# Small softmax sums for every pair of heads, and a last batch whose keys and gates stay in SBUF

## The chip, the cores and the metric

The kernel runs on one core of a Trainium2 chip. TensorE (PE in the profile) multiplies matrices into PSUM, VectorE (DVE), ScalarE (ACT) and GpSimd (POOL) do the elementwise work, and SyncE (SP) issues the transfers. The metric is the device time of one execution in microseconds; lower is better.

## The reference

Three layers follow each other on 4 batches, 12 heads, 448 tokens and 64 channels a head (768 in all).

```python
# 1. attention, for each batch and head
scores = cap * tanh(q @ k.T / 8 / cap)
attn = exp(scores - max) / (sum + 1e-9)
x = attn @ v                                  # heads side by side: [4, 448, 768]
# 2. token shift and a gated product
xk = mu_k * x + (1 - mu_k) * x_prev
xr = mu_r * x + (1 - mu_r) * x_prev
k = max(xk @ w_k, 0)                          # [4, 448, 1024], the "keys"
v = (k * k) @ w_v
x = v * sigmoid(xr @ w_r)                     # xr @ w_r are the "gates"
# 3. rotation, mixing of tokens, mixing of channels
theta = x @ w_theta
y = w_tok_r @ (x * cos(theta)) + w_tok_i @ (x * sin(theta))
u = x + y
out = u + max(u @ w_ch, 0)
```

## The kernel before

All data stand with channels on the partitions and the 448 tokens along the free axis. The products of the second and third layer are made from fp16 halves: each fp32 operand is split into a high and a low half, and three fp16 matmuls of 448 columns (high by high, high by low, low by high) stand for one product. In each batch the keys (`kmm`, 8 output tiles) and the gates (`rmm`, 6) take 6 blocks of channels each, the products with w_v (`vmm`, 6 tiles) take 8, `thm` (w_theta, 6 tiles) 6, `tmm` (tokens, 6 tiles) 7, `cmm` (w_ch, 6 tiles) 6.

Attention runs over 24 pairs of heads, pair g in batch g // 6. `scores` makes the scores, `tanh` and `exp`; `attend` adds up the four blocks of keys, divides, and splits the result into the halves that `kmm` and `rmm` read. There are two ways to divide, switched by `WIDE = 12`:

- `narrow`, pairs 0 to 11: 16 small matmuls of 112 columns sum the weights of one head and one quarter of the tokens each, so that one tile of 112 columns holds all sums (8 groups of 16 rows). VectorE takes the reciprocal of 112 columns, and 4 matmuls of 112 columns (`spread`) hand each quarter back to all channels. The output of `av` is copied to SBUF (`avo`) and multiplied there.
- `wide`, pairs 12 to 23: two additions on half the partitions each (`fold`) bring in the last block of keys, two matmuls of 448 columns give each channel its sum, VectorE takes the reciprocal of 448 columns, and one instruction multiplies the output of `av` by it straight from PSUM.

A weight matrix comes in as float64 words and goes through `group` (or `tokens` for the two token matrices): a load into one of the two buffers `w_s`; `rebase` and three bit operations that make an fp32 tile `f` (`f_s` has 3 such tiles; `tokens` uses 7 of the 9 tiles `xf_s`); `squares`, an ACT instruction that sums the squares for the scale and writes its unused output into the load buffer `w`; a small matmul, three tiny operations; and the two halves (`whi`, `wlo`).

The keys and gates of every batch are stored to DRAM (`kd`, `zd`). `values(b)` later loads the keys back through the four tiles `ka_s`, splits them into `k2_s` (8 tiles), multiplies them by w_v, loads the gates through the five tiles `z_s`, applies the sigmoid, multiplies, and stores the result to DRAM (`xd`). The products with w_v are taken in the order of the batches 0, 1, 2, 3.

`Plan` orders all this before anything runs: each operation has a rank, one or more engines with a planned duration, and the buffers it reads and writes; `order` simulates the engines, always takes the ready operation of least rank, and writes out one fixed order of instructions for each engine. A pool made with `fifo` hands out its buffers in the order in which the program names them. `o_r2`, `o_l2` mark the points where the memory of attention, and later of the first products, is given to new tiles: `o_r2` waits for the last multiplication of attention, `o_l2` for the last key and gate product.

Of the kernel before, what the change touches and what calls it, by code (L numbers as in the profile page):

```python
# [7 lines left out]
F32 = mybir.dt.float32  # L8
# [16 lines left out]
SH = S // 2  # L25
SQ = S // 4
# [4 lines left out]
KT = 7  # L31
# [217 lines left out]
def v1(n):  # L249
    return 0.17 + n / 940.0  # L250
# [6 lines left out]
def act(n):  # L257
    return 0.17 + n / 1150.0
# [19 lines left out]
def body(nc, tc, exact, qk, v, cap, mu_k, mu_r, w_k, w_v, w_r, w_th, w_tr, w_ti, w_ch, out):  # L278
# [4 lines left out]
    WIDE = 12  # L283
# [80 lines left out]
    wk, wr, wv, wt, wc = ([Buf() for _ in range(n)] for n in (1, 1, 2, 1, 1))  # L364
    wo = [Buf() for _ in range(KT)]
# [149 lines left out]
    def group(rank, src, dst, m, inv, nb, after=(), early=False):  # L515
# [44 lines left out]
    for b in range(B):  # L560
        R = (2 * NP * b - 7.1) * SLOT if b else 3
        vb = v[NP * b:NP * b + NP].rearrange("g p n -> (g p n)").rearrange("(p n) -> p n", p=128)
        parts = []
        n = 2 * DM
        for c in range(2):
            t = Buf(w_s)
            op("DMA", 0.03 + n / 700, R - 10, lambda t=t, c=c, vb=vb: nc.sync.dma_start(out=t.t, in_=vb[:, c * n:(c + 1) * n]), w=[t], after=[o_open1], name="ldm")
            parts.append([(t, lambda t=t: t.t, n, 128)] if b == 0 else (t, lambda t=t: t.t, n, t))
# [100 lines left out]
    def narrow(A, x, sxb, th, vn, z, sp, rs, ps):  # L669
# [11 lines left out]
        op("PE", 0.74, A, sums, r=[z, th[3]], w=[sp], name="sums")  # L681
# [11 lines left out]
        op("PE", 0.8, A + 2, spread, r=[rs], w=[sp], name="spread")  # L693
# [12 lines left out]
    def wide(A, x, sxb, th, vn, z, sp, ps):  # L706

        rs = lambda: x.t[:, 1:S + 1]

        def sums():  # L710
            for h in range(2):
                nc.tensor.matmul(sp.t[64 * h:64 * h + 64, 0:S], unit.to_broadcast([128, D]), z.t[:, h], start=True, stop=True, skip_group_check=True)  # L712
        op("PE", 0.74, A, sums, r=[z], w=[sp], name="sums")

        def den():
            if exact:
                nc.vector.tensor_scalar(out=rs(), in0=sp.t[:, 0:S], scalar1=1e-9, scalar2=None, op0=ALU.add)
            nc.vector.reciprocal(out=rs(), in_=rs() if exact else sp.t[:, 0:S])  # L718
        op("DVE", 2.95, A + 1, den, r=[sp], w=[x], name="den")

        def av():
            for c in range(3):
                for h in range(2):
                    nc.tensor.matmul(ps.t[64 * h:64 * h + 64, 0:S], vn.t[0][:, h, c], th[c].t[:, h], start=(c == 0), stop=False, skip_group_check=True)  # L724
            for i in range(2):
                for h in range(2):
                    nc.tensor.matmul(ps.t[64 * h:64 * h + 64, SH * i:SH * i + SH], vn.t[1][:, i, h], th[3].t[:, h], start=False, stop=True, skip_group_check=True)
        op("PE", 3.02, A + 0.5, av, r=[vn, *th], w=[ps], name="av")
        last1.append(op("DVE", v1(S) + 0.06, A + 4, lambda: nc.vector.scalar_tensor_tensor(
            out=x.t[:, 1:S + 1], in0=ps.t[:, 0:S], scalar=sxb.t, in1=rs(), op0=ALU.mult, op1=ALU.mult), r=[ps, sxb], w=[x], name="norm"))  # L730

    def attend(g):
# [8 lines left out]

        if g >= WIDE:
            for i in range(2):
                p, q = slice(64 * i, 64 * i + 64), slice(SH * i, SH * i + SH)
                op(tt(S), 0, A - 1 + 0.5 * i, lambda e, p=p, q=q: e.tensor_tensor(out=z.t[p, :, q], in0=z.t[p, :, q], in1=th[3].t[p], op=ALU.add), r=[th[3]], w=[(z, i)], name="fold")
            wide(A, x, sx[b], th, vn, z, sp, ps)
        else:
            narrow(A, x, sx[b], th, vn, z, sp, rs, ps)
# [25 lines left out]
    gone, gone_v, kend = [], [], []  # L774
# [14 lines left out]
    for b in range(B):  # L789
        def taps(i):  # L790
            return [((hi, lo), lambda hi=hi: hi.t, lambda lo=lo: lo.t) for hi, lo in (mixed[i, b, j] for j in range(KD))]
        for m, ps in units("kmm", b, wk, KF, taps(0), PAIR * NP * (b + 1), gone, PAIR * NP / 14):
            a = Buf(g_s)
            op("ACT", act(S) + 0.05, 0.0, lambda ps=ps, a=a, b=b, m=m: nc.scalar.activation(out=a.t, in_=ps.t[:, 0:S], func=AF.Relu, scale=kap[b].t[:, m:m + 1]),  # L794
               r=[ps, (kap[b], m)], w=[a], name="kev")
# [8 lines left out]
            kend.append(op("DMA", 0.65, 0.0, lambda a=a, t=kd[b][m]: nc.sync.dma_start(out=t.t, in_=a.t), r=[a], w=[kd[b][m]], name="dst"))  # L804
        for m, ps in units("rmm", b, wr, KD, taps(1), PAIR * NP * (b + 1 + KF / 14), gone, PAIR * NP / 14):
            o_ = Buf(tmp_s)
            op({"ACT": act(S), "DVE": 0.62}, 0, 0.0, lambda e, ps=ps, o_=o_: copy(e, o_.t, ps.t[:, 0:S]), r=[ps], w=[o_], name="zev")
            op("DMA", 0.65, 0.0, lambda o_=o_, t=zd[b][m]: nc.sync.dma_start(out=t.t, in_=o_.t), r=[o_], w=[zd[b][m]], name="dst")
# [7 lines left out]
    z_s, k2_s, xs_s, xg_s, xf_s, uh_s = Slots(5, True), Slots(8, True), Slots(12, True), Slots(2, True), Slots(9, True), Slots(9, True)  # L816
    CSN, ZBN, ZTN = 3, 2, 3
    cs_s, zb_s, zt_s = Slots(CSN, True), Slots(ZBN, True), Slots(ZTN, True)
    ka_s = Slots(4, True)
    q_ps, e_ps = Slots(3, True), Slots(2, True)  # L820

    def open_r2():
        live["r"].release()
        live["p"].release()
        p2 = live["p"] = tc.alloc_tile_pool(name="psum3", bufs=1, space=PSUM)
        q = tiles(p2, 4, [128, 512], F32, "q")
        q_ps.tiles, e_ps.tiles = [q[0], q[1], one[0]], q[2:]
        r2 = live["r"] = tc.alloc_tile_pool(name="r2", bufs=1, side="right")
        wt[0].tile = r2.tile([128, KD, 2, DM], F16, name="wt")
        for i, bf in enumerate(wo):  # L830
            bf.tile = r2.tile([128, 2, S], F16, name=f"wo{i}")
        ka_s.tiles = tmp2 + tiles(r2, 2, [128, S], F32, "ka")
        k2_s.tiles = tiles(r2, k2_s.n, [128, 2, S], F16, "k2")
        xf_s.tiles = tiles(r2, xf_s.n, [128, S], F32, "xf")
        xg_s.tiles = tiles(r2, xg_s.n, [128, S], F32, "xg")
# [16 lines left out]
    o_r2 = op("SYS", 0.0, 0, open_r2, after=last1)  # L852
# [10 lines left out]
    def tokens(rank):  # L863
        fo = []
        for i in range(KT):
# [12 lines left out]
            fo.append((f, fv, S, raw))  # L878
        size(rank, squares(rank, fo, small(KT)), io, 0, so)
# [52 lines left out]
    for b in range(B):  # L932
        values(b)
# [159 lines left out]
```

## Time and profile before

| | us |
|---|---|
| median of 3 runs | 805.9 (805.28 to 806.34) |
| profiled execution, its own time | 805.84 |
| its span, first to last instruction | 804.0 |
| TensorE busy | 770.6 (96% of the span) |
| VectorE busy | 563.6 (70%) |
| ScalarE busy | 440.8 (55%) |
| GpSimd busy | 92.6 (12%) |
| bytes moved by DMA | 114.76 MB, 143 GB/s on average |

The busy time of TensorE counts the full latency of each matmul, and those of neighbours overlap, so the distance between the starts of two instructions says more than the length of one. An idle time in square brackets behind an instruction names what ended it.

### The profile page before, as it was taken

What the parts mean: (1) busy time and instruction counts of PE and PEld (TensorE: products, weight loads), DVE (VectorE), ACT (ScalarE), POOL (GpSimd) and SP (SyncE); (2) the same over time, 40 slices, a digit from 0 to 9 for tenths busy, and PEclk for the clock granted to TensorE, in tenths of its full rate; (3) what the DMA queues carried; (4) which work ended last, traced back from release to release, by engine and by line L of the source; (5) the groups of instructions that cost most, each with busy time, mean ns of one, the idle gap of its engine ahead of it and who ended that gap; (6) DMA issues with size and microseconds to landing.
All of it is one profiled execution on the core that took longest, in us unless ns stands there. A gap on an engine that the chain in (4) does not pass through costs nothing.

```text
span 804.0 us, 12769 instructions
## 1 busy us (share of the span) xinstructions
PE 770.6 (96%) x4924; PEld 386.0 (48%) x4924; DVE 563.6 (70%) x1014; ACT 440.8 (55%) x677; POOL 92.6 (12%) x99
## 2 busy tenths in 40 slices
PE   5989999999999999998999889999999999999996
PEld 2445455454444444443555445555555555555553
DVE  2888897967778899879657768966856544645531
ACT  4889877878775875755526434355635333222201
POOL 1214403201130120101001000101201000000000
PEclk9999999999999999999999999999999999999999
DMA  8855455455343434225556866553535333324402
GB/s 258 257 173 181 158 180 191 138 171 184 113 136 99 139 92 157 97 75 172 176 191 221 296 193 203 185 152 84 123 60 136 82 92 92 90 65 98 99 28 73
DMA packets 116829, 114.76 MB, mean 143 GB/s; under 512 B 55820, under 2 KB 108824, under 8 KB 116760
## 3 DMA queue, kind: packets, MB, share of 16 engines
q1 hardware_dynamic: 116592, 113.86, 46.8%
q8 instruction: 40, 0.66, 0.3%
q14 instruction: 29, 0.24, 0.1%
q10 hardware_dynamic: 168, 0.01, 0.0%
HBM read 78.98 MB, written 23.86 MB: 128 GB/s over the span
## 4 chain that ended last, share of the span: by engine, by line
PE 87%; DMA 5%; DVE 4%; ACT 2%; issue 1%; SPq 1%; ACTq 0%; DVEq 0%
PE one L783 12%; PE one L784 11%; PE one L785 11%; PE big L653 7%; PE q L989 4%; PE q L987 4%; PE q L988 4%; PE one L724 4%; PE one L1010 3%; PE one L1009 3%; PE one L1011 3%; PE one L698 3%; PE q L957 2%; PE q L959 2%; PE q L958 2%; DMA w<-in_v 2%
## 5 line engine op out<-in xcount | busy, mean ns | idle before, releaser
L662 ACT ACTIVATE th<-big,tsc 128x896 f32<-128x896 f32 x72 | 70.1, 1002 | 22.6 <-PE big L653 22.4
L653 PE MATMUL big<-qk 64*64 64x448 f32 x576 | 67.8, 571 | 8.2 <-DMA qk<-in_qk 7.7
L783 PE MATMUL one<-k,wv 128*128 128x448 f16 x192 | 68.3, 356 | 6.2 <-DVE z L909 6.2
L666 ACT ACTIVATE th<-th,cap_t 128x896 f32<-128x896 f32 x72 | 73.0, 1039 | 0.0
L783 PE MATMUL one<-sl,wk 128*128 128x448 f16 x192 | 68.5, 357 | 2.4 <-ACT g L794 1.9
L784 PE MATMUL one<-sl,wk 128*128 128x448 f16 x192 | 68.2, 355 | 0.9 <-POOL sl L758 0.9
L784 PE MATMUL one<-k,wv 128*128 128x448 f16 x192 | 68.2, 355 | 0.0
L785 PE MATMUL one<-k,wv 128*128 128x448 f16 x192 | 68.1, 355 | 0.0
L785 PE MATMUL one<-sl,wk 128*128 128x448 f16 x192 | 68.1, 355 | 0.0
L989 PE MATMUL q<-wo,zt 128*128 128x448 f16 x168 | 59.2, 352 | 0.0
L987 PE MATMUL q<-wo,zt 128*128 128x448 f16 x168 | 59.2, 352 | 0.0
L988 PE MATMUL q<-wo,zt 128*128 128x448 f16 x168 | 59.2, 352 | 0.0
L1013 ACT ACTIVATE z<-one,scal 128x448 f32<-128x448 f32 x24 | 15.1, 627 | 71.9 <-PE one L1011 71.9
L783 PE MATMUL one<-sl,wr 128*128 128x448 f16 x144 | 50.9, 354 | 0.0
L785 PE MATMUL one<-sl,wr 128*128 128x448 f16 x144 | 50.7, 352 | 0.0
L784 PE MATMUL one<-sl,wr 128*128 128x448 f16 x144 | 50.7, 352 | 0.0
L973 DVE SCALAR_TENSOR_TENSOR cs<-xf,scal,cs 128x896 f32<-128x896 f32 x24 | 27.6, 1150 | 31.6 <-DMA xf<-xd 24.2
L718 DVE RECIPROCAL xt<-one 128x448 f32<-128x448 f32 x12 | 35.5, 2956 | 14.0 <-PE one L712 14.0
L758 POOL TENSOR_TENSOR sl<-mx,sl 128x448 f16<-128x448 f32 x24 | 29.5, 1230 | 119.2 <-ACT sl L294 100.6
L454 ACT ACTIVATE w<-w 128x768 f32<-128x768 f32 (+2 forms) x26 | 21.4, 823 | 35.0 <-DMA w<-in_w_ch 17.4
L1014 DVE TENSOR_TENSOR xf<-z,xf 128x448 f32<-128x448 f32 x24 | 15.0, 624 | 34.4 <-ACT z L1013 34.2
L991 DVE SCALAR_TENSOR_TENSOR xf<-q,scal,xf 128x448 f32<-128x448 f32 x24 | 16.4, 683 | 31.8 <-PE q L989 31.6
(191 smaller groups left out, 1739.5 us busy)
## 6 DMA issues: line engine op xcount, KB each, us to landing
qk<-in_qk SPq DMA_DIRECT2D x23, 448.0 KB, 3.8
kd<-g SPq DMA_DIRECT2D x32, 224.0 KB, 2.0
vn<-in_v SPq DMA_DIRECT2D x24, 256.0 KB, 2.7
w<-in_v SPq DMA_DIRECT2D x8, 768.0 KB, 6.2
w<-in_w_k SPq DMA_DIRECT2D x8, 768.0 KB, 5.1
w<-in_w_v SPq DMA_DIRECT2D x12, 512.0 KB, 4.4
zd<-tmp SPq DMA_DIRECT2D x24, 224.0 KB, 2.6
z<-zd SPq DMA_DIRECT2D x24, 224.0 KB, 2.9
```

Source lines behind the costliest of these rows:

```text
L653: nc.tensor.matmul(ps.t[o, h, 0:S], t.t[p, 1, 128 * c + 64 * i:128 * c + 64 * i + 64], t.t[p, 0], start=True, stop=True)
L662: op("ACT", act(n * S) + 0.08, A + 1 + 1.8 * c, lambda src=src, th=th: nc.scalar.activation(out=th.t, in_=src(), func=AF.Tanh, scale=tsc), ...
L666: op("ACT", act(n * S) + 0.08, A + 3 + 1.8 * c, lambda th=th: nc.scalar.activation(out=th.t, in_=th.t, func=AF.Exp, scale=cap_t), w=[th], ...
L718: nc.vector.reciprocal(out=rs(), in_=rs() if exact else sp.t[:, 0:S])
L724: nc.tensor.matmul(ps.t[64 * h:64 * h + 64, 0:S], vn.t[0][:, h, c], th[c].t[:, h], start=(c == 0), stop=False, skip_group_check=True)
L758: op(tt(S, True), 0, R + i, lambda e, t=t, hi=hi, lo=lo: e.tensor_tensor(out=lo.t, in0=t.t, in1=hi.t, op=ALU.subtract), r=[t, hi], w=[lo], ...
L783: nc.tensor.matmul(ps.t[:, 0:S], wh, xh(), start=(kk == 0), stop=False)
L784: nc.tensor.matmul(ps.t[:, 0:S], wh, xl(), start=False, stop=False)
L785: nc.tensor.matmul(ps.t[:, 0:S], wl, xh(), start=False, stop=(kk == len(xs) - 1))
L987: nc.tensor.matmul(o, z.t[:, 0, i], wo[i].t[:, 0], start=(i == 0), stop=False)
L988: nc.tensor.matmul(o, z.t[:, 1, i], wo[i].t[:, 0], start=False, stop=False)
L989: nc.tensor.matmul(o, z.t[:, 0, i], wo[i].t[:, 1], start=False, stop=(i == KT - 1))
```

## The change

- `wide` and `WIDE` go. `narrow` is renamed `normal` and serves all 24 pairs. Its planned durations are 0.36 us for the sums and 0.47 us for `spread`, where both were larger.
- The keys of batch 3 stay in SBUF: tiles 0 to 3 in `g_s`, tiles 4 to 7 in `ka_s`. Its gates stay in `xf_s`. Their stores to and loads from DRAM go. To have these tiles, `open_r2` and its mark `o_r2` move up in the program, and the key and gate evacuations of batch 3 wait for `o_r2`.
- The products with w_v are taken in the order 3, 0, 1, 2.
- `squares` writes its unused output into the two halves of the weight tile that are filled afterwards, and no longer into the load buffer, so `w` is free after the third bit operation. For w_theta and the token matrices it now waits for `o_r2`, for w_ch for `o_l2`.

```diff
+K2N = 8
...
-    WIDE = 12
...
-    def squares(rank, parts, d):
+    def squares(rank, parts, d, after=()):
         ps = Buf(c_ps)
-        for a, (f, val, n, dead) in enumerate(parts):
-            op("ACT", act(n) + 0.19, rank, lambda a=a, val=val, n=n, dead=dead: nc.scalar.activation(out=dead.t[:, 0:n], in_=val(), func=AF.Square, accum_out=d.t[:, a:a + 1]),
-               r=[f] if f is not dead else [], w=[dead, (d, a)], name="norm")
+        for a, (f, val, n, dead, place) in enumerate(parts):
+            op("ACT", act(n) + 0.19, rank, lambda a=a, val=val, place=place: nc.scalar.activation(out=place(), in_=val(), func=AF.Square, accum_out=d.t[:, a:a + 1]),
+               r=[f] if f not in dead else [], w=[*dead, (d, a)], after=after, name="norm")
...
-            parts.append((f, val, n, 128 if early else w))
-        size(rank, grams(rank, [parts], small()) if early else squares(rank, parts, small(len(parts))), inv, m, sw)
+            parts.append((f, val, n, 128) if early else (f, lambda val=val: val().rearrange("p (i t n) -> p i t n", i=nb, t=2), n, [(dst[a], (m, 0)), (dst[a], (m, 1))],
+                                                                     lambda a=a: dst[a].t[:, :, :, 128 * m:128 * m + 128].bitcast(F32)))
+        size(rank, grams(rank, [parts], small()) if early else squares(rank, parts, small(len(parts)), after), inv, m, sw)
...
-    def narrow(A, x, sxb, th, vn, z, sp, rs, ps):
+    def normal(A, x, sxb, th, vn, z, sp, rs, ps):
-        op("PE", 0.74, A, sums, r=[z, th[3]], w=[sp], name="sums")
+        op("PE", 0.36, A, sums, r=[z, th[3]], w=[sp], name="sums")
-        op("PE", 0.8, A + 2, spread, r=[rs], w=[sp], name="spread")
+        op("PE", 0.47, A + 2, spread, r=[rs], w=[sp], name="spread")
...
-    def wide(A, x, sxb, th, vn, z, sp, ps):
...
-        if g >= WIDE:
...
-            wide(A, x, sx[b], th, vn, z, sp, ps)
-        else:
-            narrow(A, x, sx[b], th, vn, z, sp, rs, ps)
+        normal(A, x, sx[b], th, vn, z, sp, rs, ps)
...
+    k2_s, xf_s, ka_s = Slots(K2N, True), Slots(9, True), Slots(4, True)
+    kept, gate = [], []
...
+    o_r2 = op("SYS", 0.0, 0, open_r2, after=last1)
...
-            a = Buf(g_s)
+            last = b == B - 1
+            a = Buf(ka_s if last and m > 3 else g_s)
...
-            kend.append(op("DMA", 0.65, 0.0, lambda a=a, t=kd[b][m]: nc.sync.dma_start(out=t.t, in_=a.t), r=[a], w=[kd[b][m]], name="dst"))
+            if last:
+                kept.append(a)
+            else:
+                op("DMA", 0.65, 0.0, lambda a=a, t=kd[b][m]: nc.sync.dma_start(out=t.t, in_=a.t), r=[a], w=[kd[b][m]], name="dst")
...
-            o_ = Buf(tmp_s)
+            o_ = Buf(xf_s if last else tmp_s)
...
+            if last:
+                gate.append(o_)
...
-            fo.append((f, fv, S, raw))
-        size(rank, squares(rank, fo, small(KT)), io, 0, so)
+            fo.append((f, lambda f=f: f.t.rearrange("p (t n) -> p t n", t=2), S, [(wo[i], 0), (wo[i], 1)], lambda i=i: wo[i].t.bitcast(F32)))
+        size(rank, squares(rank, fo, small(KT), [o_r2]), io, 0, so)
...
-    def values(b):
+    def values(b, n):
...
-            a, k = Buf(ka_s), Buf(k2_s)
+            a, k = Buf(ka_s) if n else kept[m], Buf(k2_s)
...
-            z = Buf(z_s)
+            z = Buf(z_s) if n else gate[m]
...
-    for b in range(B):
-        values(b)
+    for turn, b in enumerate((B - 1, *range(B - 1))):
+        values(b, turn)
```

## Rows read from the trace of the kernel before

**Rows 1.** The page's first part: busy us (share of the span) xinstructions.

```profile
PE 770.6 (96%) x4924; PEld 386.0 (48%) x4924; DVE 563.6 (70%) x1014; ACT 440.8 (55%) x677; POOL 92.6 (12%) x99
```

**Rows 2.** Windows by stage: length, busy PE, PEld, DVE, ACT, POOL, PEclk, DMA share, GB/s.

```profile
189.90:363.40 173.50, 172.58 (x1117) 76.10 (x1117) 143.55 (x214) 119.96 (x187) 24.62 (x21) 1.00 0.37 118
363.40:416.70 53.30, 50.19 (x260) 25.91 (x259) 39.65 (x77) 25.02 (x51) 3.59 (x3) 0.97 0.51 170
416.70:486.60 69.90, 62.31 (x332) 32.85 (x330) 48.76 (x105) 32.35 (x54) 5.92 (x9) 0.98 0.74 249
...
545.00:797.90 252.90, 252.90 (x1339) 130.83 (x1336) 135.65 (x205) 87.44 (x136) 10.20 (x6) 1.00 0.37 87
```

**Rows 3.** Waits of PE: us in total, times, longest.

```profile
PE one L783 <- DVE z L909: 6.2, 3, 2.9
...
PE one L783 <- ACT g L794: 1.9, 3, 1.6
PE one L500 <- ACT w L495: 1.4, 1, 1.4
...
PE one L712 <- DVE xt L718: 0.9, 1, 0.9
PE one L784 <- POOL sl L758: 0.9, 1, 0.9
...
PE one L783 <- ACT sl L294: 0.4, 1, 0.4
```

**Rows 4.** Timeline of PE: narrow sums and spread of one pair, then wide sums.

```profile
114.96 0.59 PE L676 MATMUL one<-pz,ones 128*32 128x112 f32 x16
115.36 0.57 PE L680 MATMUL one<-tl,ones 128*32 128x112 f32 x16
115.86 0.36 PE L783 MATMUL one<-sl,wk 128*128 128x448 f16 x1
...
118.71 1.04 PE L692 MATMUL one<-rs,row 128*128 128x112 f32 x8
119.59 0.35 PE L783 MATMUL one<-sl,wk 128*128 128x448 f16 x1
...
223.50 0.97 PE L712 MATMUL one<-pz,unit 128*64 128x448 f32 x4
224.40 0.36 PE L783 MATMUL one<-sl,wk 128*128 128x448 f16 x1
```

**Rows 5.** Groups of VectorE: the two reciprocals.

```profile
L718 DVE RECIPROCAL xt<-one 128x448 f32<-128x448 f32 x12 | 35.5, 2956 | 14.0 <-PE one L712 14.0
...
L687 DVE RECIPROCAL rs<-one 128x112 f32<-128x112 f32 x12 | 10.2, 852 | 2.9 <-PE one L680 2.7
```

**Rows 6.** Timeline of all engines, 363 to 375: the last pair's division and what follows.

```profile
363.54 2.96 DVE L718 RECIPROCAL xt<-one 128x448 f32<-128x448 f32 x1 [1.44 <-PE one L712]
...
368.33 0.68 DVE L755 SCALAR_TENSOR_TENSOR mx<-mx,mu,xt 128x448 f32<-128x448 f32 x1
...
373.94 0.58 PE L784 MATMUL one<-sl,wk 128*128 128x448 f16 x1
...
374.31 0.58 PE L785 MATMUL one<-sl,wk 128*128 128x448 f16 x1
```

**Rows 7.** Timeline of all engines, 466 to 485: a late load of w_ch.

```profile
468.34 0.38 SPq L530 DMA_DIRECT2D w<-in_w_ch  x1
...
476.00 0.91 ACT L454 ACTIVATE w<-w 128x768 f32<-128x768 f32 x1 [5.74 <-DMA w<-in_w_ch]
...
482.07 0.67 DVE L909 SCALAR_TENSOR_TENSOR z<-one,scal,z 128x448 f32<-128x448 f32 x1
```

**Rows 8.** Waits of ACT: us in total, times, longest.

```profile
ACT z L907 <- DMA z<-zd: 25.6, 13, 4.3
...
ACT w L454 <- DMA w<-in_w_ch: 17.4, 6, 5.7
```

**Rows 9.** Instructions on xf, 380 to 470: ns min/median/max, first and last start.

```profile
L467 DVE SCALAR_TENSOR_TENSOR xf<-w,xf x7: 619/625/630, 394.6 to 422.4; 128x448 uint32<-128x448 uint32 x7
```

More of the change, by code (lines that the diff above doesn't have):

```diff
@@ L362, in body @@
     rs_s = Slots(2, True)
-    wk, wr, wv, wt, wc = ([Buf() for _ in range(n)] for n in (1, 1, 2, 1, 1))
-    wo = [Buf() for _ in range(KT)]
+    wk, wr, wv, wc = ([Buf() for _ in range(n)] for n in (1, 1, 2, 1))
     junk = cpool.tile([128, 128], BF16, name="junk")
@@ L567, in body @@
             op("DMA", 0.03 + n / 700, R - 10, lambda t=t, c=c, vb=vb: nc.sync.dma_start(out=t.t, in_=vb[:, c * n:(c + 1) * n]), w=[t], after=[o_open1], name="ldm")
-            parts.append([(t, lambda t=t: t.t, n, 128)] if b == 0 else (t, lambda t=t: t.t, n, t))
+            parts.append([(t, lambda t=t: t.t, n, 128)] if b == 0 else (t, lambda t=t: t.t, n, [t], lambda t=t: t.t))
         size(R, squares(R, parts, small(2)) if b else grams(R, parts, small()), small(), 0, sv[b])
@@ L704, in narrow @@
         last1.append(op("DVE", v1(S), A + 6, lambda: nc.vector.tensor_tensor(out=x.t[:, 1:S + 1], in0=x.t[:, 1:S + 1], in1=sp.t[:, 0:S], op=ALU.mult), r=[sp], w=[x], name="norm"))
-    def wide(A, x, sxb, th, vn, z, sp, ps):
[L708 to L730, printed above, removed]
     def attend(g):
@@ L772, in body, with open_r2 @@
     attend(NG - 1)
-    gone, gone_v, kend = [], [], []
+    gone = []
+    k2_s, xf_s, ka_s = Slots(K2N, True), Slots(9, True), Slots(4, True)
+    kept, gate = [], []
+    q_ps, e_ps = Slots(3, True), Slots(2, True)
+    wt, wo = [Buf()], [Buf() for _ in range(KT)]
+    def open_r2():
+        live["r"].release()
+        live["p"].release()
+        p2 = live["p"] = tc.alloc_tile_pool(name="psum3", bufs=1, space=PSUM)
+        q = tiles(p2, 4, [128, 512], F32, "q")
+        q_ps.tiles, e_ps.tiles = [q[0], q[1], one[0]], q[2:]
+        r2 = live["r"] = tc.alloc_tile_pool(name="r2", bufs=1, side="right")
+        wt[0].tile = r2.tile([128, KD, 2, DM], F16, name="wt")
+        for i, bf in enumerate(wo):
+            bf.tile = r2.tile([128, 2, S], F16, name=f"wo{i}")
+        ka_s.tiles = tmp2 + tiles(r2, 2, [128, S], F32, "ka")
+        k2_s.tiles = tiles(r2, k2_s.n, [128, 2, S], F16, "k2")
+        xf_s.tiles = tiles(r2, xf_s.n, [128, S], F32, "xf")
+        xg_s.tiles = tiles(r2, xg_s.n, [128, S], F32, "xg")
+    o_r2 = op("SYS", 0.0, 0, open_r2, after=last1)
     def units(name, b, w, n, xs, rank, done, step=1.0):
@@ L792, in body @@
         for m, ps in units("kmm", b, wk, KF, taps(0), PAIR * NP * (b + 1), gone, PAIR * NP / 14):
-            a = Buf(g_s)
+            last = b == B - 1
+            a = Buf(ka_s if last and m > 3 else g_s)
             op("ACT", act(S) + 0.05, 0.0, lambda ps=ps, a=a, b=b, m=m: nc.scalar.activation(out=a.t, in_=ps.t[:, 0:S], func=AF.Relu, scale=kap[b].t[:, m:m + 1]),
-               r=[ps, (kap[b], m)], w=[a], name="kev")
+               r=[ps, (kap[b], m)], w=[a], after=[o_r2] if last else [], name="kev")
             def sq(e, a=a, b=b, m=m):
@@ L815, in body @@
     T2 = 2000.0
-    z_s, k2_s, xs_s, xg_s, xf_s, uh_s = Slots(5, True), Slots(8, True), Slots(12, True), Slots(2, True), Slots(9, True), Slots(9, True)
+    z_s, xs_s, xg_s, uh_s = Slots(5, True), Slots(12, True), Slots(2, True), Slots(9, True)
     CSN, ZBN, ZTN = 3, 2, 3
     cs_s, zb_s, zt_s = Slots(CSN, True), Slots(ZBN, True), Slots(ZTN, True)
[L819 to L835, printed above, removed]
     def open_l2():
@@ L850, in open_u @@
         uh_s.tiles = [w[i // 3][:, i % 3] for i in range(6)] + [la.tile([128, 2, S], F16, name=f"f{i}_u", tag=f"f{i}") for i in range(f_s.n)]
-    o_r2 = op("SYS", 0.0, 0, open_r2, after=last1)
     o_l2 = op("SYS", 0.0, 0, open_l2, after=gone)
@@ L896, in values @@
         for m in range(KF):
-            a, k = Buf(ka_s), Buf(k2_s)
+            a, k = Buf(ka_s) if n else kept[m], Buf(k2_s)
             k2.append(((k,), lambda k=k: k.t[:, 0], lambda k=k: k.t[:, 1]))
-            rk = K20 + 100 * b + m
-            op("DMA", 0.65, rk - 100, lambda a=a, t=kd[b][m]: nc.sync.dma_start(out=a.t, in_=t.t), r=[kd[b][m]], w=[a], after=[o_r2], name="lda")
+            rk = K20 + 100 * n + m
+            if n:
+                op("DMA", 0.65, rk - 100, lambda a=a, t=kd[b][m]: nc.sync.dma_start(out=a.t, in_=t.t), r=[kd[b][m]], w=[a], after=[o_r2], name="lda")
             op(cs(S), 0, rk, lambda e, a=a, k=k, b=b: copy(e, k.t[:, 0], a.t, sa[b].t), r=[a, sa[b]], w=[(k, 0)], after=[o_r2], name="k2h")
@@ L903, in values @@
                 out=k.t[:, 1], in0=a.t, scalar=sa[b].t, in1=k.t[:, 0], op0=ALU.mult, op1=ALU.subtract), r=[a, (k, 0), sa[b]], w=[(k, 1)], name="k2l")
-        for m, ps in units("vmm", b, wv, KD, k2, VM0 + VM1 * b, []):
-            z = Buf(z_s)
-            op("DMA", 0.65, T2 - 110, lambda z=z, t=zd[b][m]: nc.sync.dma_start(out=z.t, in_=t.t), r=[zd[b][m]], w=[z], after=[o_l2], name="ldz")
-            op("ACT", act(S) + 0.1, 1605.2 + 100 * b, lambda z=z, b=b, m=m: nc.scalar.activation(out=z.t, in_=z.t, func=AF.Sigmoid, scale=rho[b].t[:, m:m + 1]),
+        for m, ps in units("vmm", b, wv, KD, k2, VM0 + VM1 * n, []):
+            z = Buf(z_s) if n else gate[m]
+            if n:
+                op("DMA", 0.65, T2 - 110, lambda z=z, t=zd[b][m]: nc.sync.dma_start(out=z.t, in_=t.t), r=[zd[b][m]], w=[z], after=[o_l2], name="ldz")
+            op("ACT", act(S) + 0.1, 1605.2 + 100 * n, lambda z=z, b=b, m=m: nc.scalar.activation(out=z.t, in_=z.t, func=AF.Sigmoid, scale=rho[b].t[:, m:m + 1]),
                r=[rho[b]], w=[z], name="sig", table="sig")
```

9 lines of the change are left out of this document (4 added, 5 removed).

## The prediction

> **What bounds the kernel now.** I read the page first: TensorE is busy in 96% of the span, VectorE in 70%, ScalarE in 55% [rows 1]. A busy TensorE need not be a full one, so I went on to the windows by stage. From 545.00 to the end of the products 1339 matmuls take 252.90 us, 0.189 us each [rows 2]; for 448 columns that is 2.37 columns a nanosecond, so at 2.4 GHz there is nothing between them. The second half of attention, 189.90 to 363.40, is as dense: 172.58 of 173.50 us, and its only wait is 0.9 us in front of the wide sums, which the reciprocal of the pair before had held up [rows 2, 3]. TensorE waits in two places. Between 363.40 and 416.70 it lacks 3.1 us, between 416.70 and 486.60 7.6 us, with VectorE busy in 48.76 of these 69.9 us [rows 2].
>
> The view of TensorE's waits puts names to them [rows 3]. In the first place they are 1.9 us for `kev` (L794), 0.9 us and 0.4 us for the halves of the last pair: with the longest pause of the first row, 1.6 us, the tail of attention makes 2.9 us. In the second they are 6.2 us in 3 pauses for the VectorE instruction that takes a product with w_v out of PSUM (L909), and 1.4 us for a `squares`. Each of the two places also ends in slow matmuls: rows 373.94 and 374.31 lie 0.37 us apart, the step of 1.2 GHz [rows 6]. Eight rows go so behind the longest pause of each place, which is why the mean clock of these windows is 0.97 and 0.98 [rows 2], so each costs another 8 x (0.37 - 0.19) = 1.45 us. All that could be won there is 2.9 + 1.45 = 4.4 us in the tail and 6.2 + 1.4 + 1.45 = 9.05 us in the products with w_v.
>
> So every microsecond of TensorE work that is added to attention counts in full, and every pause that is removed counts too. The forecast is the difference of these two.
>
> **The division of pairs 12 to 23.** The narrow sums hold TensorE from 114.96 to 115.86, 0.90 us, and their `spread` from 118.71 to 119.59, 0.88 us; the wide sums hold it from 223.50 to 224.40, 0.90 us [rows 4]. One pair thus gains 0.90 + 0.88 - 0.90 = 0.88 us of TensorE work, and 12 pairs 10.6 us. Where a switch between tile shapes adds a tenth to each pair, it is 12 us: that is the upper bound. In the other direction the nearest row is the dense step: 8 records of 112 columns at a quarter of 0.189 us are 0.38 us, 4.5 us over 12 pairs. I take 10.6, because this is the same instruction between the same neighbours.
>
> VectorE loses 2956 - 852 = 2104 ns for each reciprocal [rows 5] and the two folds. It gains nothing by that while TensorE is dense: in that window it is busy in 143.55 of 173.50 us [rows 2]. What it frees on the path is the one wait of 0.9 us [rows 3]. ScalarE takes most of the added copies (`avo`) and has room: 119.96 of 173.50 us [rows 2].
>
> **The tail of attention.** Before, the last reciprocal runs 363.54 to 366.50, the subtraction and the mix follow, the mix at 368.33, and TensorE has used up its prepared blocks by then [rows 6]. With the narrow division the two folds go, and 0.85 us plus a `spread` of 0.88 us replace 2.96 us. The keys of batch 0, which now stand in ScalarE's and VectorE's queue between the last halves and `kev`, also go from there, since batch 3 comes first. The three `squares` of w_theta that were done before the end of attention now wait for `o_r2`; they land behind it and may take some of this back. Of 4.4 us I count 3.5 as gone (bounds 0 and 4.4).
>
> **The products with w_v.** Late transfers start these pauses, and the fixed queues pass them on. The load of w_ch issued at 468.34 is waited for by the `rebase` that starts at 476.00, after 5.74 us of idle ScalarE; the pieces of the keys stand behind it, VectorE behind them, and L909 comes at 482.07, while its product had long been done [rows 7]. Over the run ScalarE waits 17.4 us for w_ch and 25.6 us for the gates coming back through the five tiles `z_s` [rows 8].
>
> Three parts of the change act on that. With `w` free after the third bit operation, the next load no longer waits for `squares`, and the transfers behind it in SP's queue come earlier too. The last batch sends no keys or gates through DRAM: 14 stores and 14 loads go from the queue. And the first batch of products needs no `z_s`, so five gates of the next can wait there in time.
>
> Two parts act against it. In a `fifo` pool the seven tiles of `tokens` now stand behind the six gates of batch 3 in `xf_s`, so this work, which began at 394.6 and was part done when the products began [rows 9], starts only when the gates are out, and its late loads fall into the products. And the planner still orders ScalarE as if a weight load came early, so a shorter cycle of `w` also puts the `rebase` earlier. Batch 0 being 27 us later (6 x 24 matmuls at 0.189), the first `thm` of batch 0, which fill holes, come later too. Of 9.05 us I count 3.0 as gone; the bounds are all of it, and a loss as large as three more pauses of the mean size, 3 x 2.1 = 6 us.
>
> **Where nothing is counted.** The keys and gates that stay save no engine time beyond the queues above: their splitting and sigmoid are the same instructions. From 545 on the same products run in the same number. The smaller planned durations of `sums` and `spread` change the order of everything, the first half too, where I have no row for it; I allow 1.5 us either way.
>
> **Sum.** The profiled execution took 805.84 us, 1.84 more than its span and practically the median of 805.9. 805.84 + 10.6 - 0.9 - 3.5 - 3.0 = 809.0 us, 0.4% slower.
>
> **Rivals.**
>
> *All pauses of the products close* (faster). The late `rebase` is the one start of most of them, and the earlier free `w` removes it. For it: the 17.4 us of waiting for w_ch [rows 8]. Against it: a transfer that takes 7 us still takes 7 us, and the tokens move in. 805.84 + 10.6 - 0.9 - 4.4 - 9.05 = 802.1 us. It decides once the products give back more than 10.6 - 0.9 - 3.5 = 6.2 us. Chance 0.20.
>
> *The token work crowds the products.* Each of its late loads holds ScalarE, VectorE behind it, and an L909. Against it: VectorE has a third of that window free [rows 2]. With three more pauses, 805.84 + 10.6 - 0.9 - 3.5 + 6 = 818.0 us. Chance 0.18.
>
> *The added sums cost TensorE nothing*, because its busy time hides room. 805.84 - 0.9 - 3.5 - 3.0 = 798.4 us. Against it stands the step of 0.189 us. Chance 0.05. The Trainium skill (Perfetto Trace Analysis, Identifying the Most-Contended Engine) says that matmul busy time is a bad measure of how near a kernel is to the roof, since matmuls overlap; by that rule 96% proves nothing. The trace agrees that the busy time alone proves nothing; the step between starts, which is what the argument uses, does not depend on it.
>
> *The spread packs at the dense step*, 0.38 us instead of 0.88: 805.84 + 4.5 - 7.4 = 802.9 us. Against it: the row of 0.88 us [rows 4]. Chance 0.03. The Trainium skill (TensorE: Matmul & The Clock Gate, Back-to-back issue gap) gives a warm matmul of N columns N / 2.4 + 2.5 ns, for 8 of 112 columns an estimate of 0.39 us. The trace differs with 0.88 us in place, and the measurement decides.
>
> That the change does not do what it says I leave out: no pair can take the wide path any more, and no transfer of the last batch's keys and gates is left.
>
> **How the numbers follow.** What the forecast holds has chance 0.54 and lies between 805 and 813. A measurement tells about 0.2% from no change, that is 804.2 to 807.5. The lower edge of the forecast and the upper edge of the first rival fall in there, 0.17 together. Faster: most of the first rival and the two small ones, 0.24. Slower: most of the forecast and the crowd, 0.59. The range goes from just above the first rival, 802.5, to 816, into the crowd; the forecast's own range is 805 to 813.
>
> **What would show it.** Right: 24 instead of 12 groups of `spread`, 0.88 us or more in place; attention's last sums about 10 us later than 363.4; a shorter pause or none at `kev`; the waits of L783 for L909 between 2 and 8 us in all; the same dense stage behind. Wrong: a window of attention's second half with gaps in TensorE; waits for L909 near zero (faster) or above 12 us (slower); another length of the first half, which would mean that the new order and not the parts decided.

## The result, and the profile after

The kernel after takes 814.6 us (median of 4 runs, 812.46 to 817.64) against 805.8 us before (805.28 to 806.34): a ratio of 1.0108, 95% interval 1.0083 to 1.0134. It is 8.8 us slower, where 3.2 us were forecast: the direction held, and so did the stated range of 802.5 to 816, but 814.6 lies 5.6 us above the forecast of 809.0 and above the forecast's own range, which ended at 813. The profiled execution is the slowest of the four (817.64 us, span 815.8), so its profile shows some 3 us more than the median. Half of that lies in the first half of attention: the `spread` of pair 11 starts at 178.2, and at 176.7 in e4 (below), which has the same instructions up to there. The mean granted clock between 48 and 52 us is 0.57 in this execution and 1.00 in that of e4.

First the page's first part of after, to be read beside [rows 1]. TensorE has 432 more matmul records. VectorE is busy for 28.0 us less.

```profile
PE 785.8 (96%) x5356; PEld 402.9 (49%) x5356; DVE 535.6 (66%) x1018; ACT 429.4 (53%) x652; POOL 92.3 (11%) x106
```

The windows of after: the four of [rows 2], and one over all of its products with w_v that have pauses.

```profile
189.90:363.40 173.50, 173.50 (x1420) 86.84 (x1417) 113.27 (x210) 111.11 (x170) 12.38 (x13) 1.00 0.39 126
363.40:416.70 53.30, 52.99 (x328) 28.25 (x327) 38.50 (x81) 28.85 (x51) 3.86 (x5) 1.00 0.18 58
416.70:486.60 69.90, 66.44 (x349) 34.70 (x348) 46.17 (x104) 27.00 (x50) 6.56 (x8) 0.98 0.56 179
545.00:797.90 252.90, 252.90 (x1339) 130.85 (x1338) 142.06 (x215) 94.35 (x146) 14.64 (x9) 1.00 0.40 93
...
427.00:522.00 95.00, 86.42 (x454) 45.34 (x453) 70.23 (x166) 39.74 (x70) 10.25 (x13) 0.97 0.69 225
```

In the second half of attention TensorE has no gap at all, and VectorE has 60 us free. From 545 on both kernels are equally dense. The lack is in the products with w_v: 8.6 us between 427 and 522.

The waits of TensorE in after, beside [rows 3] (total, times, longest). L772 to L774 stand where L783 to L785 stood, L784 is `kev`, L890 takes a product with w_v out of PSUM, L494 is `squares`:

```profile
PE one L772 <- DVE xf L890: 3.2, 3, 2.5
PE one L499 <- ACT wc L494: 2.9, 1, 2.9
...
PE one L772 <- DVE z L890: 2.4, 1, 2.4
PE one L772 <- ACT wr L494: 1.1, 1, 1.1
...
PE one L772 <- ACT g L784: 0.2, 1, 0.2
```

The waits for the last halves are gone and that for `kev` is 0.2 us. The waits for L890 make 5.6 us where L909 made 6.2 us, and two waits for `squares` make 4.0 us where one made 1.4 us (the 1.1 us for w_r lie at 149 us, in attention).

The timeline of the last pair in after, beside [rows 6]:

```profile
371.60 0.59 PE L676 MATMUL one<-pz,ones 128*32 128x112 f32 x16
...
372.64 0.86 DVE L687 RECIPROCAL rs<-one 128x112 f32<-128x112 f32 x1 [0.93 <-PE one L680]
373.18 2.48 PE L698 MATMUL one<-th,vn 128*64 128x448 f32 x12
...
376.35 1.15 PE L692 MATMUL one<-rs,row 128*128 128x112 f32 x8
...
377.33 0.35 PE L772 MATMUL one<-sl,wk 128*128 128x448 f16 x1
...
377.58 0.84 ACT L494 ACTIVATE wt<-f 128x768 f32<-128x768 f32 x1 [0.42 <-PE one L692]
...
382.04 1.01 DVE L543 SCALAR_TENSOR_TENSOR wt<-f,scal,wt 128x768 f16<-128x768 f32 x1
```

The last sums start at 371.60, 9.1 us later than in the kernel before, where the rows of PE give 362.52 for the last wide sums. The short reciprocal lies under `av`. One `spread` holds TensorE from 376.35 to 377.33. The first `squares` of w_theta (L494) comes behind the last pair, and its low half (L543) on VectorE not before 382.04.

And the late loads of the products with w_v in after, beside [rows 7]:

```profile
434.70 0.40 DVE L457 TENSOR_SCALAR w<-w 128x448 f32<-128x448 f32 x1 [6.04 <-DMA w<-in_w_tr]
...
437.02 1.26 DVE L890 SCALAR_TENSOR_TENSOR xf<-one,scal,xf 128x448 f32<-128x448 f32 x2
...
437.75 0.53 PE L772 MATMUL one<-k,wv 128*128 128x448 f16 x1 [2.53 <-DVE xf L890]
...
490.21 0.90 ACT L453 ACTIVATE w<-w 128x768 f32<-128x768 f32 x1 [4.33 <-DMA w<-in_w_ch]
...
492.67 0.83 ACT L494 ACTIVATE wc<-f 128x768 f32<-128x768 f32 x1
...
516.17 0.88 POOL L455 TENSOR_SCALAR w<-w 128x768 f32<-128x768 f32 x1 [14.47 <-DMA w<-in_w_ch]
...
517.08 0.98 DVE L460 TENSOR_SCALAR f<-w 128x768 uint32<-128x768 uint32 x1 [2.33 <-POOL w L455]
...
518.96 0.67 DVE L890 SCALAR_TENSOR_TENSOR z<-one,scal,z 128x448 f32<-128x448 f32 x1
```

Each of the three long pauses begins with a weight load that an engine waits for: a token load in front of VectorE (6.04 us), w_ch in front of ScalarE (4.33 us), w_ch in front of GpSimd (14.47 us). What stands behind in the fixed queues waits with it.

### The profile page after: what moved, and what is told of

Read it like the earlier page. It is cut to its first block, busy times and chain, and to the rows that moved or that the text cites. A ratio compares the mean times of both kernels' runs of the same rounds, so it can differ in the third digit from the quotient of the medians.

```text
span 815.8 us, 13545 instructions
## 1 busy us (share of the span) xinstructions
PE 785.8 (96%) x5356; PEld 402.9 (49%) x5356; DVE 535.6 (66%) x1018; ACT 429.4 (53%) x652; POOL 92.3 (11%) x106
## 4 chain that ended last, share of the span: by engine, by line
PE 88%; DMA 5%; ACT 2%; DVE 2%; issue 1%; SPq 0%; POOL 0%; ACTq 0%; POOLq 0%; DVEq 0%
PE one L772 12%; PE one L773 11%; PE one L774 11%; PE big L653 7%; PE one L698 6%; PE q L968 4%; PE q L969 4%; PE q L970 4%; PE one L990 3%; PE one L991 3%; PE one L992 3%; PE one L692 3%; PE q L938 2%; PE q L940 2%; PE q L939 2%; PE one L701 2%
## 5 line engine op out<-in xcount | busy, mean ns | idle before, releaser
L772 PE MATMUL one<-k,wv 128*128 128x448 f16 x192 | 68.9, 359 | 5.8 <-DVE xf L890 3.2
L774 PE MATMUL one<-k,wv 128*128 128x448 f16 x192 | 68.6, 357 | 0.0
L772 PE MATMUL one<-sl,wk 128*128 128x448 f16 x192 | 68.3, 356 | 0.2 <-ACT g L784 0.2
L774 PE MATMUL one<-sl,wk 128*128 128x448 f16 x192 | 68.1, 355 | 0.2 <-DVE wk L543 0.2
L698 PE MATMUL one<-th,vn 128*64 128x448 f32 x288 | 59.4, 548 | 0.0
L772 PE MATMUL one<-sl,wr 128*128 128x448 f16 x144 | 50.9, 354 | 1.2 <-ACT wr L494 1.1
L774 PE MATMUL one<-sl,wr 128*128 128x448 f16 x144 | 50.7, 352 | 0.0
L991 PE MATMUL one<-w_u,wc 128*128 128x448 f16 x108 | 38.1, 352 | 0.0
L990 PE MATMUL one<-w_u,wc 128*128 128x448 f16 x108 | 38.1, 352 | 0.0
L992 PE MATMUL one<-w_u,wc 128*128 128x448 f16 x108 | 38.1, 352 | 0.0
```

Of the source, the lines that this page charges most:

```text
L772: nc.tensor.matmul(ps.t[:, 0:S], wh, xh(), start=(kk == 0), stop=False)
L774: nc.tensor.matmul(ps.t[:, 0:S], wl, xh(), start=False, stop=(kk == len(xs) - 1))
L990: nc.tensor.matmul(ps.t[:, 0:S], wh, u.t[:, 0], start=(kk == 0), stop=False)
L991: nc.tensor.matmul(ps.t[:, 0:S], wh, u.t[:, 1], start=False, stop=False)
```

## The experiments

All kernels were timed beside the kernel before on the same chip; e1 to e4, e5 to e8 and e9 to e12 ran on three different chips, so two runs are compared by the last column. "Kept batch" is that part of the change alone: batch 3 stays in SBUF and is first among the products with w_v.

| run | what it is | median us | ratio to before | 95% interval | against its own before, us |
|---|---|---|---|---|---|
| after | the whole change | 814.6 | 1.0108 | 1.0083 to 1.0134 | +8.8 |
| e1 | after, wide division back in pairs 12 to 23 | 810.5 | 1.0055 | 1.0030 to 1.0080 | +4.4 |
| e2 | before, narrow division in all pairs | 819.4 | 1.0175 | 1.0150 to 1.0201 | +13.4 |
| e3 | before, new place of `squares` | 812.2 | 1.0100 | 1.0063 to 1.0137 | +6.2 |
| e4 | after, `spread` twice in pairs 12 to 23 | 822.9 | 1.0228 | 1.0198 to 1.0259 | +16.9 |
| e5 | after, old place of `squares` | 814.7 | 1.0105 | 1.0088 to 1.0122 | +8.4 |
| e6 | before, kept batch alone | 803.5 | 0.9969 | 0.9956 to 0.9981 | -2.8 |
| e7 | kept batch, pair 23 narrow | 803.3 | 0.9957 | 0.9939 to 0.9976 | -3.0 |
| e8 | after, old planned durations | 815.7 | 1.0112 | 1.0075 to 1.0150 | +9.4 |
| e9 | kept batch, new place for w_r, w_v | 809.8 | 1.0054 | 1.0032 to 1.0077 | +3.3 |
| e10 | kept batch, new place for w_th, tokens, w_ch | 800.4 | 0.9921 | 0.9899 to 0.9942 | -6.0 |
| e11 | kept batch, wide from pair 9 | 805.7 | 0.9997 | 0.9983 to 1.0010 | -0.7 |
| e12 | kept batch, wide from pair 18 | 809.9 | 1.0054 | 1.0036 to 1.0071 | +3.5 |

**e1, the wide division put back.**

```diff
+        if g >= 12:
...
+            wide(A, x, sx[b], th, vn, z, sp, ps)
+        else:
+            normal(A, x, sx[b], th, vn, z, sp, rs, ps)
-        normal(A, x, sx[b], th, vn, z, sp, rs, ps)
```

> The changed kernel with the wide division put back for pairs 12 to 23; everything else of the change stays. Theory A (the added spread on a full TensorE is the cost, 12 us in the profile after; the small division gives back the tail of attention): 814.6 - 12 + 4.4 = 807 us, and the pauses for kev come back. Rival B (the new order, the kept batch and the moved token work cost the time, not the division): still 811 or more. Rival C (keeping the batch is itself a gain that the division hid): 803 or less.

810.5 us: 4.4 us of the 8.8 stay when the added sums are gone. So something other than the division costs time too. The interval takes in rival B's 811 and not theory A's 807, and the wait for `kev` is 0.6 us where 1.9 us stood before. The second half of attention, which is free of waits in after, has 3.8 us of them in e1, each for VectorE or ScalarE.

**e2, the division alone.**

```diff
-    WIDE = 12
+    WIDE = 24
```

> The kernel before with the small division for all 24 pairs and its own planned costs; nothing else changed. Theory A: 805.8 + 12 - 0.9 - 4.4 = 812.5 us, 24 groups of spread at about 0.9 us in place, no pause at kev. Rival B (the rest of the change is the cost): 808 or less.

819.4 us, 13.4 us slower, above both theories. The division by itself costs more than the 10.6 us that were forecast for the added `spread`, and it gives nothing back in the tail: the waits there, between 363 and 395, are 2.9 us in e2 (1.3 for `kev`, 1.0 and 0.6 for the halves) and 3.1 us before. Over the whole run:

```profile
PE one L783 <- ACT g L794: 1.5, 3, 1.2
...
PE one L784 <- POOL sl L758: 1.0, 1, 1.0
```

**e3, the new place of `squares` alone**, that is, the part of the diff in `squares`, `group` and `tokens` in the kernel before.

> The kernel before with only the new place of the unused output of squares, so that the load buffer is free after the third bit operation. Theory A: the pauses for L909 that late loads of w_ch cause shrink, 803 to 806 us. Rival B (squares now waits for the new memory and comes late): 808 or more, with pauses in front of the matmul that sums the squares.

812.2 us, 6.2 us slower, though no engine has more work. Rival B's number held, but not its reason: the longest new pause is not in front of the matmul that sums the squares, it is 1.9 us in front of a wide sum, for VectorE's fold. e9 and e10 take this apart.

**e4, a doubled `spread`.** The second set of matmuls writes the same values over the first.

```diff
+        twice = A >= 12 * PAIR + 10
...
-            for i in range(4):
+            for i in [*range(4), *range(4 * twice)]:
```

> The changed kernel with the four spread matmuls of pairs 12 to 23 issued twice (the second four write the same values again). Theory A: 12 x 0.88 = 10.6 us more than the changed kernel, 825 us. If spread packs at the dense step: 4.5 us more, 819 us. If TensorE has hidden room there: no more than 1 us, 815 us.

822.9 us, 8.1 us above after by the two differences, or 0.68 us for each of 12; the two intervals together leave some 5 to 11 us. In the groups of its profile the instruction has 96 more records (e4 first, then after), and they are 10.7 us longer, 0.89 us for each pair.

```profile
L694 PE MATMUL one<-rs,row 128*128 128x112 f32 x288 | 37.0, 278 | 0.8 <-DVE rs L687 0.8
```

```profile
L692 PE MATMUL one<-rs,row 128*128 128x112 f32 x192 | 26.3, 280 | 0.8 <-DVE rs L687 0.8
```

A `spread` is paid in full or nearly so. That ends two rivals of the forecast: that added sums cost nothing, and that they pack at 0.38 us (12 of them would be 4.5 us). Some of the 10.7 us may have come back in the products with w_v: the other instructions of e4 stand in the order of after, but in its profile the pauses there make 5.4 us, and 8.5 us in that of after.

**e5, the squares back in the load buffer**, the reverse of e3 in the kernel after.

> The changed kernel with the unused output of squares back in the load buffer (no wait for the new memory, the buffer free only after squares). Theory A (three parts that add up: the division costs about 12, the new place of squares about 6, the kept batch gives back about 9): 814.6 - 6 = 808 to 809 us. Rival B (every edit makes a new order, and the order's accidents decide; the parts do not add up): 813 or more, or below 805.

814.7 us, as after: rival B's number. Where all pairs are narrow the place of the squares makes no difference in sum. The trace shows two parts that work against each other. In the tail of attention two low halves of w_theta (L542 here) stand on VectorE ahead of the last mix (L722), and TensorE waits for the cast behind it; in after that work comes later, and this wait is gone.

```profile
376.58 1.01 DVE L542 SCALAR_TENSOR_TENSOR wt<-f,scal,wt 128x768 f16<-128x768 f32 x1
...
378.05 1.02 DVE L542 SCALAR_TENSOR_TENSOR wt<-f,scal,wt 128x768 f16<-128x768 f32 x1
378.98 0.68 DVE L722 SCALAR_TENSOR_TENSOR mx<-mx,mu,xt 128x448 f32<-128x448 f32 x1
...
380.31 0.35 PE L771 MATMUL one<-sl,wk 128*128 128x448 f16 x1 [1.26 <-ACT sl L294]
```

Between 363 and 395 the waits are 2.9 us in e5 and 0.2 us in after; between 420 and 545, in the products with w_v, they are 6.9 us in e5 and 8.5 us in after.

**e6, the kept batch alone**, with the wide division, the old squares and the old planned durations:

```diff
+            a = Buf(ka_s if last and m > 3 else g_s)
...
+            o_ = Buf(xf_s if last else tmp_s)
...
+    for turn, b in enumerate((B - 1, *range(B - 1))):
+        values(b, turn)
```

> The kernel before with only the third part of the change: the keys and gates of batch 3 stay in SBUF and its products with w_v come first; wide division for pairs 12 to 23, old place of squares, old planned costs. Theory A: 797 to 802 us, the tail of attention free of the keys of batch 0, fewer waits for the gates. Rival B, and the forecast's own picture, in which this part is worth little: 804 to 808 us.

803.5 us, 2.8 us faster than before, between theory A's 802 and rival B's 804. Behind the start its waits of TensorE have none of over 1.6 us, and `kev` (L815 here) holds it for 0.3 us in all:

```profile
PE one L803 <- DVE xf L921: 2.0, 3, 1.6
...
PE one L804 <- DVE sl L757: 1.1, 1, 1.1
...
PE one L803 <- ACT sl L294: 0.4, 1, 0.4
...
PE one L803 <- ACT g L815: 0.3, 2, 0.2
```

The pause at `kev` thus goes with the keys of batch 0 and needs no shorter division. (It is not gone in every order: in e5, which keeps the batch too, a `kev` is waited for again, 1.3 us in all.) With the same squares, e5 against e6 is the price of 12 narrow pairs and the two planned durations: 8.4 + 2.8 = 11.2 us.

**e7, the last pair alone narrow.**

```diff
-        if g >= 12:
+        if 12 <= g < NG - 1:
```

> As the run before this one, with the small division for the last pair alone (pair 23), so that its chain to the first product is shorter. Theory A: 0.9 us of TensorE work against up to 4 us of pauses in the tail, 1 to 3 us less than the run before. Rival B: no difference that can be told from noise.

803.3 us, as e6. In its trace the waits for the last halves fall from 1.1 + 0.4 = 1.5 us (e6) to 0.6 us, and one `spread` of 0.9 us is added: the two cancel.

**e8, the old planned durations** (0.74 and 0.8) in the kernel after.

> The changed kernel with the planned durations of before for the sums and the spread (0.74 and 0.8 us in place of 0.36 and 0.47); the work is the same, only the order differs. Theory A: 813 to 816 us. Rival B (the order counts as much as the work): 3 us or more away from 814.6.

815.7 us, not to be told from after. The 1.5 us that were allowed for this part are not seen, though the two intervals would hide 3 us. So the 11.2 us above are put down to the division; that the planned durations have no share in them is not shown.

**e9 and e10, the place of the squares in two halves.** Both start from e6. e9 moves the squares of w_r and w_v, whose buffers come free early in attention; e10 those of w_th, the tokens and w_ch, which then wait for `o_r2` or `o_l2`. e9's edit:

```diff
-            parts.append((f, val, n, 128) if early else (f, val, n, [w], lambda w=w: w.t[:, 0:n]))
+            parts.append((f, val, n, 128) if early else (f, lambda val=val: val().rearrange("p (i t n) -> p i t n", i=nb, t=2), n, [(dst[a], (m, 0)), (dst[a], (m, 1))],
+                                                                     lambda a=a: dst[a].t[:, :, :, 128 * m:128 * m + 128].bitcast(F32)) if (inv is ir or inv is iv) else (f, val, n, [w], lambda w=w: w.t[:, 0:n]))
...
```

> The kept batch with the wide division of the kernel before, and the new place of the squares for w_r and w_v alone (their load buffers come free early in attention; nothing waits for the new memory). Theory (the early freed buffers bring the bits of weights into a VectorE that is nearly full in the second half of attention with the wide division): 808 to 811 us. Rival (the squares that wait for the memory of attention crowd its tail): about 803.5, as with the squares left where they were.

> The kept batch with the wide division, and the new place of the squares for w_th, the tokens and w_ch alone (these wait for the memory that attention leaves). Theory (early buffers crowd VectorE): 803 to 805 us. Rival (squares that wait for the new memory crowd the tail of attention): 808 to 811.

e9 takes 809.8 us, 6.1 us more than e6; e10 takes 800.4 us, 3.2 us less than e6 and the best of all. The first theory's number held for e9, and the rival fell: squares that wait for the new memory do not crowd the tail, they clear it. The theory had not foreseen that gain; it had 803 to 805 us for e10. The timeline of e9 around its longest pause in attention's second half:

```profile
288.28 0.75 DVE L543 SCALAR_TENSOR_TENSOR wv<-f,scal,wv 128x512 f16<-128x512 f32 x1
...
289.54 0.75 DVE L543 SCALAR_TENSOR_TENSOR wv<-f,scal,wv 128x512 f16<-128x512 f32 x1
290.20 0.62 DVE L758 TENSOR_TENSOR sl<-mx,sl 128x448 f16<-128x448 f32 x1
290.74 1.09 DVE L739 TENSOR_TENSOR pz<-pz,th 128x896 f32<-128x896 f32 x1
...
292.00 2.84 POOL L745 TENSOR_TENSOR pz<-pz,tl 64x448 f32<-64x448 f32 x2 [6.40 <-DVE pz L739]
292.38 1.46 DVE L745 TENSOR_TENSOR pz<-pz,tl 64x448 f32<-64x448 f32 x1
...
293.98 0.97 PE L712 MATMUL one<-pz,unit 128*64 128x448 f32 x4 [1.95 <-DVE pz L745]
```

VectorE goes without a break from one instruction to the next, two halves of w_v stand in front of the fold (L745), and the wide sums wait 1.95 us for it. Of that, 0.84 us may be the fold's own: it takes 1.46 us while GpSimd folds too, where it takes 0.62 us at 363.58. Then the tail of e9 and that of e10:

```profile
363.58 0.62 DVE L745 TENSOR_TENSOR pz<-pz,tl 64x448 f32<-64x448 f32 x1
...
374.36 1.02 DVE L543 SCALAR_TENSOR_TENSOR wt<-f,scal,wt 128x768 f16<-128x768 f32 x1
375.30 0.68 DVE L755 SCALAR_TENSOR_TENSOR mx<-mx,mu,xt 128x448 f32<-128x448 f32 x1
...
376.62 0.35 PE L804 MATMUL one<-sl,wk 128*128 128x448 f16 x1 [2.18 <-ACT sl L294]
```

```profile
369.44 0.63 DVE L751 TENSOR_TENSOR mx<-xt 128x448 f32<-128x448 f32 x1
370.17 1.41 DVE L755 SCALAR_TENSOR_TENSOR mx<-mx,mu,xt 128x448 f32<-128x448 f32 x2
...
373.36 0.35 PE L805 MATMUL one<-sl,wk 128*128 128x448 f16 x1 [0.17 <-POOL sl L758]
373.70 1.41 DVE L543 SCALAR_TENSOR_TENSOR wt<-f,scal,wt 128x768 f16<-128x768 f32 x1
```

In e9 the low half of w_theta (L543) stands on VectorE ahead of the last mix (L755), and TensorE waits 2.18 us. In e10 it cannot be ready so soon, comes after the mixes, and the wait is 0.17 us. The kernel after has this order too, and e5 shows the other one beside the narrow division.

**e11 and e12, the price by pair.** The wide division starts at pair 9 or at pair 18 of e6.

```diff
-        if g >= 12:
+        if g >= 9:
```

> The kept batch with the squares where they were, and the wide division from pair 9 instead of pair 12: three spread packs fewer. Theory (TensorE is the limit of attention, and a spread group costs its full 0.9 us on it): 803.5 - 3 x 0.9 = about 800.8 us. Rival (VectorE, which divides three more wide rows, becomes the limit of those pairs): 803.5 to 807.

> The kept batch with the squares where they were, and the wide division only from pair 18: six spread packs more than in the kept batch alone. Theory (each spread costs 0.9 us on a full TensorE, pair by pair): 803.5 + 6 x 0.9 = about 809 us. Rival (the price lies in the last pairs, where the tail is): about 803.5 to 805.

e12 costs 6.3 us over e6 for 6 pairs, 1.05 us each: pair by pair, as the theory had it. e11 gains nothing; its 805.7 us are 2.1 us more than e6. That lies in the rival's range, but the trace doesn't show the rival's reason: in the view of TensorE's waits no wide sum of e11 waits for a fold or a reciprocal. Its last sums start at 357.46 against 362.14 in e6. Some of these 4.7 us are work that only moved behind the sums, but the three `spread` are gone. What they gave was lost again: behind the start, the longest wait of e11 is in the tail, for the same cast (L294) that cost e6 0.4 us.

```profile
PE one L803 <- ACT sl L294: 3.2, 1, 3.2
PE one L803 <- DVE xf L921: 3.0, 3, 2.6
```

In front of that wait two low halves of w_theta stand on VectorE (L542, at 366.99 and 368.46, ahead of the last mixes at 370.04 and 370.76), as in e9. Neither of the two stated reasons was right here.

## Why the prediction was right, and which sizes were off

**The division, 10.6 us: right in kind, 1.5 us short together with the wait.** TensorE is full in attention and each `spread` counts. Less the 0.9 us of the wait in front of the wide sums, 9.7 us were on the sum; with the squares held fixed it is 11.2 us (e5 against e6). The row taken, 0.88 us, is the shortest step that a `spread` takes: in after seven of the twelve added ones hold TensorE for 0.88 us and five for 0.97 to 0.98 us, 0.92 us in the mean. With the sums (0.91 us narrow, 0.88 us wide) that is 0.95 us a pair and 11.4 us of added work in the trace, so the upper bound of 12 us was nearer than 10.6. In device time the price hangs on what stands beside it: 13.4 us without the kept batch (e2), 4.4 us beside the new squares (after against e1), where the wide pairs of e1 stand in pauses that the narrow ones don't have.

The Trainium skill (TensorE: Matmul & The Clock Gate, LDWEIGHTS) puts a weight load at its columns divided by 1.2 in ns. For the 8 loads of 128 columns of one `spread` that is an estimate of 0.85 us. The trace of after comes near it: the loads take 0.97 us of the 0.98 us that the step lasts, so they fill it. The 0.38 us of the rival counted the columns of the matmuls and left the loads out.

```profile
376.34 0.97 PEld L692 LDWEIGHTS one<-rs,row 128*128 128x128 f32 x8 [0.33 <-DVE sl L726]
```

**The tail, 3.5 of 4.4 us: the size was right, the cause was not.** Of 2.9 us of waits 0.2 us are left, and no slow rows follow, so 4.2 us went. But the shorter division is not what took them: e6 takes `kev` away with the wide division, e2 with the narrow one alone keeps 2.9 us of waits there, and e7 gains nothing. Of the two causes the prediction had named the order of the batches (e6); the other is the squares of w_theta behind `o_r2` (e10 beside the wide division, after against e5 beside the narrow one). The prediction feared that these would "take some of this back"; that was the wrong sign. That the size came out is luck: one cause too many was counted, and one was counted as a loss.

**The products with w_v, 3.0 us given back: the term that was most off, by how much is open.** In the profiled execution the waits there are 3.2 + 2.4 + 2.9 = 8.5 us, and two groups of 8 matmuls behind 437.75 and 519.69 go at half speed for another 3.0 us: 11.5 us where 9.05 us were, 2.4 us lost and not 3.0 us won. Some of these 5.4 us belong to this one execution, which is 3 us above the median: e4, with the same order of instructions but for the doubled `spread`, has 5.4 us of waits there in its profile, 1.6 us below its median, and a granted clock of 1.00 from 420 to 545, which would be a gain of some 3.6 us. So nearly the same order gives a loss in one execution and a gain in another, and what this term is at the median is open. The reason given, that a load buffer which is free earlier brings the loads and the transfers behind them earlier, did not work. The three late loads are still waited for, one is now a token load, and the rival about the token work named that mechanism, with 6 us as its price. Taken by itself the early freeing of w_r's and w_v's buffers costs 6.1 us beside the wide division (e9). Its weight work takes its turns on a VectorE that the wide pairs had busy in 143.55 of 173.50 us [rows 2]. That this is the whole of the 6.1 us is not shown: the pauses named above make 1.95 us and, in the tail, 1.8 us more than in e6, and slow rows follow two of e9's pauses. How much of it remains beside the narrow division was not run apart; e5 shows only that early and late part together come to nothing there, with 2.7 us less of waits in the tail and 1.6 us more in the products.

**The sum by measured parts:** 805.8 - 2.8 (kept batch, e6) + 11.2 (division, e5 less e6) + 0.4 (squares, after less e5) = 814.6 us. This closes by construction, as each part is the step from one run to the next; another order of the steps gives the parts other sizes (the division 4.4 to 13.4 us, the squares 6.2 us in e3 and 0.4 us here). On the forecast's side stood 9.7 us of loss and 6.5 us of gain; by these steps it is 11.2 us and 2.4 us. The larger part of the miss, 4.1 of 5.6 us, is gain that did not come, and as the tail gave its 4.2 us in the trace, it is missing elsewhere, by that trace in the products with w_v above all.

**The rivals.** All pauses closed: no, three long ones stay. Token work crowds the products: in part, one of the three; the 814.6 us lie nearer to its 818.0 than to the forecast's 809.0, and that the stated range held them is owed to the share of this rival in it. Added sums for nothing, or at the dense step: no (e4, e12). Of the signs named, 24 `spread` groups, last sums about 10 us later (9.1), no pause at `kev`, L890 between 2 and 8 us (5.6) and the same dense stage came as said. Of the opposite signs, the first half is 1.5 us longer in this execution, but not in e4, so the order didn't lengthen it.

**The better version** is e10: the kept batch, the wide division from pair 12, and the new place for the squares of w_th, the tokens and w_ch alone. It takes 800.4 us, 0.9921 of before (0.9899 to 0.9942).

## What to carry to other kernels

On an engine whose starts have no gap, added work is paid in full, and its size is better taken from the mean over all of its groups with the step to the next instruction than from one neat row: the twelve `spread` of the kernel before take 0.88 to 1.08 us, 0.97 us in the mean, and the row taken was 0.88 us. A pause is credited to the part that moves the work standing in the waiting queue, and that is found by listing what is queued ahead of the late instruction, not by shortening the last link. A buffer that comes free earlier is no gain by itself: its next load brings work to some engine, and in front of a full one that work displaces something on the path, as e9 shows; the same edit where the work lands behind the path gained 3.2 us (e10).

## What the runs showed of the hardware

A `spread` is filled by its weight loads, 0.97 us for 8 in after, and not by its columns: four fp32 records of 448 columns, twice as many columns as its eight of 112, hold TensorE for 0.90 us in the wide sums [rows 4]. Of two folds that VectorE and GpSimd ran at the same time in e9, one was slow: at 292.38 VectorE's took 1.46 us, at 348.11 it took 0.62 us and GpSimd's, begun 0.04 us later, 1.58 us, against 0.62 us (363.58) and 1.13 us (283.58) without the other's. The matmuls behind a pause of TensorE of 2.5 us went at half speed for 8 rows; the rows of PE in after show the steps:

```profile
437.75 0.53 PE L772 MATMUL one<-k,wv 128*128 128x448 f16 x1 [2.53 <-DVE xf L890]
438.07 0.58 PE L773 MATMUL one<-k,wv 128*128 128x448 f16 x1
438.45 0.58 PE L774 MATMUL one<-k,wv 128*128 128x448 f16 x1
438.82 0.58 PE L772 MATMUL one<-k,wv 128*128 128x448 f16 x1
```

They start 0.37 us apart, the step of 1.2 GHz. The wait of 2.88 us that ends at 493.6 in the same execution was not followed by such rows, so a pause of that length doesn't always cost it. In e6, whose longest pause in the tail and the products is 1.6 us, the granted clock is 1.00 from 362 to 545. Runs of one kernel lay further apart here than those of before: 804.95 to 815.44 us in e1 against 803.19 to 808.63 us beside it. Whether the slow rows make that spread is not shown, as each kernel has one profile.
